# Retention and rational feed-forward on one core: a limit of three loads ahead on SyncE's queue, from the fifteenth load on

## The chip, the core and the metric

One core of a Trainium2 chip runs the whole program. The metric is the device time of one execution in microseconds (us); of several runs the median counts. The trace comes from one execution, taken by the hardware profiler.

## What is computed

The reference is decay-weighted attention without a softmax (retention), followed by a feed-forward layer whose activation is a quotient of a cubic and a quadratic. All is float32.

```python
# q, k, v: 8 batches, 8 heads, 576 positions, head size 64
gamma = 1.0 - 2.0 ** (-5.0 - np.arange(H))
rel = pos[:, None] - pos[None, :]
Dmat = np.where(rel >= 0, gamma[:, None, None] ** rel[None], 0.0)
x = ((q @ k.T) / 8 * Dmat) @ v          # (4608, 512) after the heads are joined
h = x @ w_in                            # 512 -> 2048
P = a[0] + a[1] * h + a[2] * h**2 + a[3] * h**3
Q = 1.0 + abs(b[0]) * abs(h) + abs(b[1]) * h**2
out = (P / (Q + 1e-6)) @ w_out          # 2048 -> 512
```

## The kernel before

The 4608 rows are cut into 36 **units** of 128 rows. A unit needs two loads: `qk` (queries and keys, 512 KB) and `kv` (keys and values, 512 KB; for units 0 to 3 only the values, 256 KB). Nine units make up two batches, and a state `S` is carried from unit to unit. The feed-forward layer works on nine blocks of 512 rows by sixteen slices of the hidden layer, one slice per **step**, 144 steps in all: `gemm1` (tiles `h`), the elementwise chain on ScalarE and VectorE (tiles `u`, `v`, `p`, `g`), then `gemm2` (tiles `acc`).

The weights come as 32 loads of 512 KB (`bits0_f` for slice f of `w_in`, `bits1_f` for slice f of `w_out`). Their words are taken apart and split into parts by ScalarE, VectorE and GpSimd some steps before a slice is first used.

Units 0 to 3 are worked on before the first step (`before(n)`), and unit 4 is begun there. After that a **visit** `visit(a, k)` finishes unit a and begins unit k: (4, 5) in step 0, (5, 6) in step 2, (6, 7) in step 4, the end of unit 7 in step 6, unit 8 from step 23 on, then a visit every two steps (24, 26, 28, 30) and from step 30 on every four. In a visit the matmuls read `qk` and `kv` of both units. Where the two halves of the TensorE array write one PSUM bank, the visit lets a matmul wait until the other half's matmuls are done. It does so through SyncE: an instruction that only waits is put on SyncE's queue and waits for TensorE, and a later matmul waits for it:

```python
            if n in after:
                seen[after[n]] = follow(nc.sync.nop(), ins)
```

So SyncE's queue holds three kinds of things, worked off strictly in order: the loads, the stores of finished output rows (`store`), and these waiting instructions (line 379). Each engine's own order is written out by hand in the tables `BEFORE0` and following. For SyncE it is not: its instructions come from the scheduler, which sets a load where it thinks that the load's buffer and semaphore are free.

The loads share eight semaphores in turn (`DMAHW0` to `DMAHW7`), so each DMA already waits until the DMA eight places ahead of it on the queue has landed.

The loads are called for in this order: constants, unit 0, masks, unit 1, mask, `bits0_0`, units 2 and 3, `bits0_1`, `bits0_2` (these are fourteen), then `bits0_3`, unit 4, `bits1_0`, `bits0_4`, unit 5, `bits1_1`, `bits0_5`, unit 6, and then two weights per step with the units between them as their buffers come free (`done_with`), until `bits1_15`; after that only units.

Of the kernel before, what the change touches and what calls it, by code (L numbers as in the profile page):

```python
# [21 lines left out]
P = 128  # L22
B, H, S, D = 8, 8, 576, 64
# [3 lines left out]
NPAIR = H // 2  # L27
# [44 lines left out]
VISITS |= {24 + 2 * i: (8 + i, 9 + i) for i in range(3)}  # L72
VISITS |= {30 + 4 * i: (11 + i, 12 + i if i < 24 else None) for i in range(25)}
WARM = "8 3 0 0 0 0 0 0 0".split()
LN_SHIFT = 60


# [12 lines left out]
def retention_ffn(ctx: ExitStack, tc: tile.TileContext, qkv, w_in, w_out, consts, masks, out):  # L90
# [10 lines left out]
    nc = tc.nc  # L101
# [19 lines left out]

    raws = {}

    def load_unit(n):


        late = 2 <= n < 6
        pools = [(wts, f"w{w}_{10 + n}") if late else (raw, "qk" if w == 0 else "kv") for w in range(2)]
        qk = pools[0][0].tile([P, 2, NPAIR, P], F32, tag=pools[0][1], name=f"qk{n}")
        nc.sync.dma_start(qk, qkv[n, :, 0:1024].rearrange("p (a g i) -> p a g i", a=2, g=NPAIR))  # L130
        kv = pools[1][0].tile([P, 2, H, D], F32, tag=pools[1][1], name=f"kv{n}")
        a = 1 if n < NP else 0
        nc.sync.dma_start(kv[:, a:], qkv[n, :, 1024 + 512 * a : 2048].rearrange("p (a h d) -> p a h d", h=H, d=D))
        raws[n] = qk, kv

    const_sb = const.tile([P, NPAIR * P + H + NPAIR + 6], F32, name="const_sb")
# [3 lines left out]
    mask_sb = const.tile([P, D], F32, name="mask_sb")  # L140
    firsts = op.tile([P, 2, DM], F32, tag="o0", name="whole_sb")[:, 0, 0 : 2 * P]
# [7 lines left out]
    def warm(n, by=None):  # L149
        by = gq_sb[:, 0] if by is None else by  # L150
        for _ in range(n):
            pe.matmul(unread[:, 0:P], by, by, start=True, stop=True)

    warm(int(WARM[0]), zeros)
    a0, a1, a2, a3 = (ab_sb[:, i : i + 1] for i in range(4))
# [4 lines left out]
    bits = {}  # L160
# [4 lines left out]
    def load_weight(k):  # L165

        bits[k] = wts.tile([P, DM], I64, tag=f"w{k[0]}_{k[1]}", name=f"bits{k[0]}_{k[1]}")
        nc.sync.dma_start(bits[k], (w_in, w_out)[k[0]][k[1]])

    def split_weight(k):  # L170

# [166 lines left out]
    def whole_outputs(n):  # L338
        q, v, o = raws[n][0][:, 0], raws[n][1][:, 1], sums_of(n)
        for j in range(2):  # L340
            ret = whole_ret(n, j)
            for c in range(2):
                for e in range(2):
                    pe.matmul(o[e * D : (e + 1) * D, j, c, :], v[:, 4 * c + 2 * e + j, :], ret[:, 2 * c + e, :], start=c == 0, stop=True, skip_group_check=True)
        if n % 9:
            for c in range(2):
                for j in range(2):
                    for e in range(2):
                        r = slice(j * D, j * D + D)
                        pe.matmul(o[e * D : (e + 1) * D, j, c, :], state[n][r, 2 * c + e, :], q[r, 2 * c + e, :], start=False, stop=True, skip_group_check=True)  # L350
# [30 lines left out]
    def follow(ins, earlier):  # L381
        how = mybir.DependencyInfo(mybir.DependencyClass.Sync, mybir.DependencyReason.DATA)
        tc.add_manual_dep(ins.ins, earlier.ins.name, how, reason="rows of the array that write one bank")
        return ins
# [20 lines left out]
    def done_with(a):  # L405

        del raws[a]
        state.pop(a, None)
        if 6 <= a + 2 < NU:
            load_unit(a + 2)  # L410
# [105 lines left out]
    def ffn_r(b, f):  # L516

        u, v, p = els[b, f]
        act.activation(u, v, AF.Ln, bias=math.ldexp(QC, -LN_SHIFT), scale=math.ldexp(1.0, -LN_SHIFT))
        act.activation(u, u, AF.Exp, bias=-LN_SHIFT * math.log(2.0), scale=-1.0)  # L520

# [132 lines left out]
    def load_weights(n):  # L654
        for k in [k for _, k in zip(range(n), loads)]:
            load_weight(k)
# [12 lines left out]
    def run(names, todo):  # L669
        todo |= {f"split{j}": (split_step, j) for j in range(4)}  # L670
        for name in names:
            if name in todo:
                todo[name][0](*todo[name][1:])

    def before(n):
        def outputs():
            if n == 1:
                nc.sync.dma_start(mask_sb, masks[:, 2 * P :])
            whole_outputs(n - 1)
            done_with(n - 1)  # L680
            load_more(n)

        todo = {"start": (split_start, int(STARTS_BEFORE[n]))}
        todo |= {f.__name__: (f, n + 1) for f in (scale_q, scale_v)}
        if n < NP:
            todo |= {"scores": (whole_scores, n), "state": (whole_state, n), "add": (whole_add, n), "fade": (fade, n)}
            todo |= {"decay": (whole_decay, n, 0), "decay1": (whole_decay, n, 1)}
            todo |= {"turn": (turn, n), "kn": (keep_turned, n)}
            todo["warm_a"] = warm, int(WARM[n + 1])
        else:  # L690
            todo |= {"scores": (visit, None, n), "decay": (decay, n), "add": (add, n), "fade": (fade, n)}
        if n >= 1:
            todo |= {f.__name__: (f, n - 1) for f in (keep_hi, keep_lo)}
            todo["outputs"] = (outputs,)
            if n < NP:
                todo["warm_b"] = warm, int(WARM[n + 5])
        run((BEFORE0, BEFORE1, BEFORE2, BEFORE3, BEFORE4)[n], todo)
# [4 lines left out]
    def load_more(n):  # L702


        for what in loading:
            if what == "|":
                return
            load_weights(1) if what == "weight" else load_unit(next(units))

    nc.sync.dma_start(const_sb, consts)  # L710
    load_unit(0)
    nc.sync.dma_start(firsts, masks[:, 0 : 2 * P])
    load_more(0)
    scale_q(0)
    scale_v(0)
# [12 lines left out]
    for i in range(len(steps) + lag(len(steps))):  # L728
# [4 lines left out]
        if i in VISITS:  # L733
            a, k = VISITS[i]
# [64 lines left out]
```

## Time and profile before

| | us |
|---|---|
| median of 3 runs | 868.04 |
| lowest and highest run | 867.76, 870.98 |
| the profiled execution | 871.07 |
| span of its trace | 869.0 |

The 2.07 us between the profiled execution's time and its span lie outside the instructions. The profiled execution is 3.03 us over the median.

### The profile page before, as it was taken

Reading aid. Unit: us, or ns where it says so; the run is one execution under the profiler, and the core shown is the slowest. Engines: PE = TensorE matmul, PEld = TensorE weight load, DVE = VectorE, ACT = ScalarE, POOL = GpSimd, SP = SyncE. Lnnn points to the kernel's source line nnn. Section 1 sums busy time; section 2 is a strip of 40 time slices with the busy share of each in tenths; the row PEclk is TensorE's granted clock in tenths of the full one; section 3 lists DMA queues with packets and bytes.
Section 4 is the critical chain, followed back from the end, with each engine's and each line's share of the span. In section 5 each row is a group of like instructions: output and inputs, shape, how many; then the busy total and the mean of one; then the engine's idle time right before and its main releaser. Section 6 shows DMA issues by size and latency. Waiting matters only on the chain.

```text
span 869.0 us, 18739 instructions
## 1 busy us (share of the span) xinstructions
PE 849.4 (98%) x7574; PEld 727.2 (84%) x7574; DVE 773.4 (89%) x1221; ACT 665.6 (77%) x1240; POOL 130.8 (15%) x107
## 2 busy tenths in 40 slices
PE   8899999999999999999999999999999999999997
PEld 6666787778888888888888888888888888888886
DVE  4998999999899889888889888888898988888995
ACT  3888999988767778777877787777877787767775
POOL 2523333631001110111111100011111111000000
PEclk9999999999999999999999999999999999999999
DMA  9896000032121112111211121101211121001001
GB/s 341 320 340 232 1 2 0 1 99 101 48 98 50 49 50 98 49 50 50 97 50 50 50 89 60 47 30 37 87 47 50 49 98 50 1 2 48 1 1 48
DMA packets 20774, 64.55 MB, mean 74 GB/s; under 512 B 2512, under 2 KB 2640, under 8 KB 20688
## 3 DMA queue, kind: packets, MB, share of 16 engines
q1 hardware_dynamic: 20528, 63.10, 20.6%
q8 instruction: 59, 0.97, 0.4%
q14 instruction: 27, 0.22, 0.1%
q10 hardware_dynamic: 160, 0.26, 0.1%
HBM read 53.91 MB, written 9.44 MB: 73 GB/s over the span
## 4 chain that ended last, share of the span: by engine, by line
PE 83%; DVE 10%; ACT 4%; issue 1%; DMA 1%; SPq 0%; POOL 0%; ACTq 0%; DVEq 0%; POOLq 0%
PE acc L86 39%; PE h L86 36%; DVE p L86 4%; PE ps L86 4%; DVE v L86 3%; PE y L86 2%; DVE c L86 1%; ACT free_at L86 1%; PE psNone L86 1%; DMA qk<-in_qkv 1%; ACT bits L86 1%; ACT g L86 1%; ACT c L86 0%; DVE qk L86 0%; ACT p L86 0%
## 5 line engine op out<-in xcount | busy, mean ns | idle before, releaser
L86 PE MATMUL h<-xhi,w 128*128 128x512 f32 x1152 | 367.8, 381 | 3.8 <-DVE p L86 1.9
L86 PE MATMUL acc<-w,g 128*128 128x512 f32 x1584 | 366.9, 381 | 3.0 <-ACT o L86 1.6
L86 PEld LDWEIGHTS acc<-w,g 128*128 128x128 f32 x1584 | 296.5, 189 | 47.6 <-ACT o L86 2.0
L86 PEld LDWEIGHTS h<-xhi,w 128*128 128x128 f32 x1152 | 217.7, 189 | 37.9 <-DVE p L86 3.1
L86 ACT ACTIVATE p<-h,const_sb 128x512 f32<-128x512 f32 x144 | 111.6, 775 | 165.0 <-PE h L86 158.4
L86 PE MATMUL h<-xlo,w 128*128 128x512 f32 x576 | 218.4, 379 | 0.1
L86 DVE TENSOR_TENSOR p<-p,h 128x512 f32<-128x512 f32 x144 | 98.6, 684 | 42.5 <-ACT u L86 40.1
L86 PEld LDWEIGHTS h<-xlo,w 128*128 128x128 f32 x576 | 108.9, 189 | 16.7 <-issue 1.1
L86 DVE SCALAR_TENSOR_TENSOR p<-p,const_sb,h 128x512 f32<-128x512 f32 x144 | 107.3, 745 | 4.0
L86 ACT ACTIVATE v<-u,absb 128x512 f32<-128x512 f32 x129 | 103.2, 800 | 0.4 <-DVE p L86 0.2
L86 DVE TENSOR_TENSOR v<-v,u 128x512 f32<-128x512 f32 x131 | 101.4, 774 | 0.2 <-ACT v L86 0.2
L86 DVE SCALAR_TENSOR_TENSOR p<-v,p 128x512 f32<-128x512 f32 x140 | 98.6, 704 | 3.3
L86 DVE SCALAR_TENSOR_TENSOR p<-p,const_sb,u 128x512 f32<-128x512 f32 x131 | 99.2, 758 | 1.2 <-ACT u L86 1.2
L86 POOL TENSOR_TENSOR S<-S,const_sb 128x256 f32<-128x256 f32 x32 | 27.2, 850 | 453.4 <-DVE S L86 453.4
L86 DVE SCALAR_TENSOR_TENSOR v<-v,u 128x512 f32<-128x512 f32 x131 | 89.4, 683 | 0.0
L86 ACT ACTIVATE u<-u 128x512 f32<-128x512 f32 x131 | 82.6, 630 | 4.3
L86 ACT ACTIVATE g<-p 128x512 fp32r<-128x512 f32 x132 | 82.8, 627 | 3.5 <-DVE p L86 3.0
L86 ACT ACTIVATE u<-v 128x512 f32<-128x512 f32 x131 | 81.9, 625 | 0.8 <-DVE v L86 0.8
L86 DVE TENSOR_TENSOR g<-p,g 128x512 fp32r<-128x512 f32 x115 | 78.6, 683 | 0.7 <-ACT g L86 0.7
L86 ACT ACTIVATE u<-h 128x512 f32<-128x512 f32 x131 | 76.7, 585 | 2.5 <-DVE v L86 2.4
L86 ACT ACTIVATE kv<-kv,const_sb 128x64 f32<-128x64 f32 x232 | 58.2, 333 | 4.5 <-DMA kv<-in_qkv 4.5
L86 POOL TENSOR_TENSOR qk<-qk,const_sb 128x512 f32<-128x512 f32 x31 | 48.6, 1566 | 38.8 <-DMA qk<-in_qkv 38.7
(93 smaller groups left out, 713.7 us busy)
## 6 DMA issues: line engine op xcount, KB each, us to landing
qk<-in_qkv SPq DMA_DIRECT2D x36, 512.0 KB, 4.1
kv<-in_qkv SPq DMA_DIRECT2D x32, 512.0 KB, 5.5
bits<-in_w_in SPq DMA_DIRECT2D x16, 512.0 KB, 8.1
bits<-in_w_out SPq DMA_DIRECT2D x16, 512.0 KB, 7.3
out<-o SPq DMA_DIRECT2D x28, 256.0 KB, 3.7
kv<-in_qkv SPq DMA_DIRECT2D x4, 256.0 KB, 7.0
out<-o SPq DMA_DIRECT2D x8, 128.0 KB, 2.1
out<-last SPq DMA_DIRECT2D x2, 256.0 KB, 2.4
```

Source lines behind the costliest of these rows:

```text
L86: return lambda *a, **k: self.tc.keep_in_program_order(method(*a, **k))
```

## The change

Every load, and only loads, goes through one helper. From the fifteenth call on, a load gets a dependence on the third load called for ahead of it: SyncE holds it back until that one has landed.

```diff
+AHEAD = 3
+FREE = 14
...
+    begun = []
+
+    def load(to, source):
+
+        begun.append(nc.sync.dma_start(to, source))
+        if len(begun) > FREE:
+            follow(begun[-1], begun[-1 - AHEAD])
+
...
-        nc.sync.dma_start(qk, qkv[n, :, 0:1024].rearrange("p (a g i) -> p a g i", a=2, g=NPAIR))
+        load(qk, qkv[n, :, 0:1024].rearrange("p (a g i) -> p a g i", a=2, g=NPAIR))
...
-        nc.sync.dma_start(bits[k], (w_in, w_out)[k[0]][k[1]])
+        load(bits[k], (w_in, w_out)[k[0]][k[1]])
```

The constants, the masks and `kv` go through it in the same way; the stores do not. `follow` (line 380) adds the dependence and is not changed.

**The first held-back loads.** On SyncE's queue, before, from the fourteenth load (`bits0_2`) to unit 5; the names in brackets are the semaphores that a row waits for:

```order
L168 DMA bits0_2_187<-in_w_in 128x512 [waits DMAHW5_49]
L168 DMA bits0_3_249<-in_w_in 128x512 [waits DMAHW6_49]
L130 DMA qk4_251<-in_qkv 128x1024 [waits DMAHW7_49]
L133 DMA kv4_253<-in_qkv 128x1024 [waits DMAHW0_49]
L168 DMA bits1_0_255<-in_w_out 128x512 [waits DMAHW1_49]
L168 DMA bits0_4_257<-in_w_in 128x512 [waits DMAHW2_49]
L130 DMA qk5_259<-in_qkv 128x1024 [waits DMAHW3_49]
L133 DMA kv5_261<-in_qkv 128x1024 [waits DMAHW4_49]
```

And the same place now, where all loads have the helper's line:

```order
L130 DMA bits0_2_187<-in_w_in 128x512 [waits DMAHW5_49]
L130 DMA bits0_3_249<-in_w_in 128x512 [waits DMAHW6_49,DMAHW3_49]
L130 DMA qk4_251<-in_qkv 128x1024 [waits DMAHW7_49,DMAHW4_49]
L130 DMA kv4_253<-in_qkv 128x1024 [waits DMAHW5_49,DMAHW0_49]
L130 DMA bits1_0_255<-in_w_out 128x512 [waits DMAHW6_49,DMAHW1_49]
L130 DMA bits0_4_257<-in_w_in 128x512 [waits DMAHW7_49,DMAHW2_49]
L130 DMA qk5_259<-in_qkv 128x1024 [waits DMAHW0_49]
L130 DMA kv5_261<-in_qkv 128x1024 [waits DMAHW1_49]
```

The order is the same here; `bits0_3` now also waits for `kv3`, `qk4` for `bits0_1`, `kv4` for `bits0_2`, and so on, each for the third ahead.

**The loads around the visit of step 4.** On SyncE's queue, before, from `bits0_8` on; a weight load that names `PE_49` stands right behind the waiting instructions of a visit:

```order
L168 DMA bits0_8_857<-in_w_in 128x512 [waits DMAHW3_49]
L168 DMA bits0_9_859<-in_w_in 128x512 [waits DMAHW4_49]
L168 DMA bits0_10_907<-in_w_in 128x512 [waits DMAHW5_49]
L168 DMA bits0_11_909<-in_w_in 128x512 [waits DMAHW6_49]
L168 DMA bits1_8_986<-in_w_out 128x512 [waits DMAHW7_49]
L168 DMA bits0_12_988<-in_w_in 128x512 [waits PE_49,DMAHW0_49,DVE_49]
L168 DMA bits1_9_1041<-in_w_out 128x512 [waits DMAHW1_49]
L130 DMA qk8_813<-in_qkv 128x1024 [waits DMAHW2_49,DVE_49,PE_49]
L133 DMA kv8_815<-in_qkv 128x1024 [waits DMAHW3_49,DVE_49,Pool_49]
```

And now:

```order
L130 DMA bits0_8_857<-in_w_in 128x512 [waits DMAHW2_49]
L130 DMA bits0_11_909<-in_w_in 128x512 [waits DMAHW3_49]
L130 DMA bits1_8_986<-in_w_out 128x512 [waits PE_49,DMAHW4_49]
L130 DMA qk8_813<-in_qkv 128x1024 [waits DMAHW0_49,DVE_49,PE_49]
L130 DMA kv8_815<-in_qkv 128x1024 [waits DMAHW1_49,DVE_49,Pool_49]
L130 DMA bits0_13_1043<-in_w_in 128x512 [waits DMAHW5_49]
L130 DMA bits0_9_859<-in_w_in 128x512 [waits DMAHW6_49]
L130 DMA bits0_10_907<-in_w_in 128x512 [waits DMAHW7_49]
L130 DMA bits1_11_1130<-in_w_out 128x512 [waits DMAHW0_49]
L130 DMA bits1_13_1183<-in_w_out 128x512 [waits DMAHW3_49,Activation_49]
L130 DMA qk9_962<-in_qkv 128x1024 [waits PE_49,DVE_49,DMAHW1_49,Pool_49]
```

Here loads have changed places: `bits0_9` and `bits0_10`, whose third load ahead is `qk8` and `kv8`, now stand behind that unit. The visit of step 6 has its waiting instruction between `bits1_13` and `qk9` now, and had it just ahead of `bits1_13` before.

**Who waits for SyncE.** On TensorE the order has not changed. In the visit (5, 6) of step 2 two matmuls wait for SyncE's waiting instructions, the second of them here (lines of the kernel before):

```order
L86 MATMUL ps5_6_569<-kv6_489 64x64 [waits SP_sequencer_49]
L86 MATMUL ps5_6_569<-kv6_489 64x64
L86 MATMUL y6_570<-kv6_489 64x64 x2
L86 MATMUL ps5_6_569<-kv6_489 64x64 x2
L86 MATMUL y6_570<-kv6_489 64x64 x2
L86 MATMUL ps5_6_569<-kv6_489 64x64 x2
L86 MATMUL y6_570<-kv6_489 64x64 x2
L86 MATMUL ps5_6_569<-kv6_489 64x64 x2
L86 MATMUL ps5_6_569<-qk5_259,kv5_261 64x64 [waits SP_sequencer_49]
```

On VectorE, ScalarE and GpSimd, too, the order is the same as before; only the numbers of the load semaphores differ.

## Rows read from the trace of the kernel before

**Rows 1.** The page: busy time by engine; DMA busy tenths in 40 slices.
```profile
PE 849.4 (98%) x7574; PEld 727.2 (84%) x7574; DVE 773.4 (89%) x1221; ACT 665.6 (77%) x1240; POOL 130.8 (15%) x107
DMA  9896000032121112111211121101211121001001
```

**Rows 2.** Waits (us, times, longest), whole span; the last three lie within 0-14 us.
```profile
POOL qk L86 <- DMA qk<-in_qkv: 38.7, 2, 19.4
...
POOL kv L86 <- DMA kv<-in_qkv: 10.9, 2, 9.4
...
DVE qk L86 <- DMA qk<-in_qkv: 8.4, 3, 4.6
...
ACT kv L86 <- DMA kv<-in_qkv: 4.5, 1, 4.5
```

**Rows 3.** Timeline of SyncE's queue: issue time, us, what (kv3, bits0_1 to 3, qk4, ...).
```profile
6.95 0.51 SPq L133 DMA_DIRECT2D kv<-in_qkv  x1
9.06 1.45 SPq L168 DMA_DIRECT2D bits<-in_w_in  x3
11.07 0.33 SPq L130 DMA_DIRECT2D qk<-in_qkv  x1
...
31.57 0.33 SPq L133 DMA_DIRECT2D kv<-in_qkv  x1
...
32.42 0.42 SPq L168 DMA_DIRECT2D bits<-in_w_in  x1
...
55.72 0.33 SPq L168 DMA_DIRECT2D bits<-in_w_in  x1
```

**Rows 4.** Landing, us after issue: windows around the six issues above; last two 230-860.
```profile
kv<-in_qkv SPq DMA_DIRECT2D x1, 256.0 KB, 8.4
...
bits<-in_w_in SPq DMA_DIRECT2D x1, 512.0 KB, 7.6
...
qk<-in_qkv SPq DMA_DIRECT2D x1, 512.0 KB, 9.8
...
kv<-in_qkv SPq DMA_DIRECT2D x1, 512.0 KB, 4.4
...
bits<-in_w_in SPq DMA_DIRECT2D x1, 512.0 KB, 6.4
...
bits<-in_w_in SPq DMA_DIRECT2D x1, 512.0 KB, 4.2
...
qk<-in_qkv SPq DMA_DIRECT2D x22, 512.0 KB, 4.0
kv<-in_qkv SPq DMA_DIRECT2D x22, 512.0 KB, 5.4
```

**Rows 5.** Timelines of VectorE and GpSimd: first uses of qk2, qk4, kv4, qk5, kv5.
```profile
12.33 0.69 DVE L86 TENSOR_TENSOR qk<-qk,const_sb 128x512 f32<-128x512 f32 x1 [1.04 <-DMA qk<-in_qkv]
...
21.45 1.73 POOL L86 TENSOR_TENSOR qk<-qk,const_sb 128x512 f32<-128x512 f32 x1
...
23.13 1.49 POOL L86 TENSOR_TENSOR kv<-kv,const_sb 128x512 f32<-128x512 f32 x1
25.99 0.93 POOL L86 TENSOR_TENSOR S<-S,const_sb 128x256 f32<-128x256 f32 x1 [1.37 <-DVE S L86]
...
28.57 0.68 DVE L86 TENSOR_TENSOR qk<-qk,const_sb 128x512 f32<-128x512 f32 x1
...
31.07 0.68 DVE L86 TENSOR_TENSOR kv<-kv,const_sb 128x512 f32<-128x512 f32 x1
```

**Rows 6.** TensorE's timeline at step 2; the chain that ended last at step 6.
```profile
42.91 0.67 PE L86 MATMUL ps<-qk,kv 64*64 64x64 f32 x16
...
71.14 0.02 SPq L379
```

**Rows 7.** SyncE's own waits, 20 to 76 us: for TensorE in the visits.
```profile
SPq L379 <- PE ps L86: 25.0, 5, 10.1
```

**Rows 8.** Timeline of ScalarE: first use of bits0_9.
```profile
98.01 0.86 ACT L86 ACTIVATE c<-bits 128x512 f32<-128x512 f32 x1
```

More of the change, by code (lines that the diff above doesn't have):

```diff
@@ L129, in load_unit @@
         qk = pools[0][0].tile([P, 2, NPAIR, P], F32, tag=pools[0][1], name=f"qk{n}")
-        nc.sync.dma_start(qk, qkv[n, :, 0:1024].rearrange("p (a g i) -> p a g i", a=2, g=NPAIR))
+        load(qk, qkv[n, :, 0:1024].rearrange("p (a g i) -> p a g i", a=2, g=NPAIR))
         kv = pools[1][0].tile([P, 2, H, D], F32, tag=pools[1][1], name=f"kv{n}")
         a = 1 if n < NP else 0
-        nc.sync.dma_start(kv[:, a:], qkv[n, :, 1024 + 512 * a : 2048].rearrange("p (a h d) -> p a h d", h=H, d=D))
+        load(kv[:, a:], qkv[n, :, 1024 + 512 * a : 2048].rearrange("p (a h d) -> p a h d", h=H, d=D))
         raws[n] = qk, kv
@@ L677, in outputs @@
             if n == 1:
-                nc.sync.dma_start(mask_sb, masks[:, 2 * P :])
+                load(mask_sb, masks[:, 2 * P :])
             whole_outputs(n - 1)
@@ L708, in load_more @@
             load_weights(1) if what == "weight" else load_unit(next(units))
-    nc.sync.dma_start(const_sb, consts)
+    load(const_sb, consts)
     load_unit(0)
-    nc.sync.dma_start(firsts, masks[:, 0 : 2 * P])
+    load(firsts, masks[:, 0 : 2 * P])
     load_more(0)
```

## The prediction

> **What bounds the kernel now.** I read the page first. TensorE is busy for 849.4 of 869.0 us, and VectorE for 773.4; the DMA engines are full only in the first four slices, some 87 us, and mostly below a third from then on [rows 1]. So a change of the loads can matter in two ways only: an engine waits for a load, or an engine waits for SyncE, whose queue holds the loads.
>
> The list of waits answers the first. Four lines name a load. Those of ScalarE, of VectorE, and of GpSimd for `kv` all lie in the first 14 us and are for units 0 to 2, whose loads are among the first fourteen and are not touched. The largest line, 38.7 us in two pieces, is GpSimd with nothing else to do (it is busy for 130.8 us in all) late in the kernel [rows 1, 2]. After 14 us nothing on the way to the end waits for a load. So there is no DMA wait to remove, and the question is how much room the loads have to be later.
>
> **What the change does to a load.** Before, up to eight loads are on their way. A load's landing is its issue [rows 3] plus its time to landing [rows 4]: kv3 lands at 6.95 + 8.4 = 15.35, bits0_1 at 9.06 + 7.6 = 16.66, qk4 at 11.07 + 9.8 = 20.87. Between bits0_1 and qk4 stand two more loads, so one of 512 KB lands every (20.87 - 16.66) / 3 = 1.40 us. The long time to landing of 8 to 10 us is therefore queueing behind the loads ahead: the engines take them one after the other. Holding a load back until two are ahead of it takes away waiting in the DMA queue and adds the same waiting on SyncE, as long as two loads keep the DMA engines busy while the third is being started.
>
> So one number decides, the time L from issue to landing with two loads ahead. The trace does not show it. From below: a load can land no faster than one issued alone, 4.0 us (22 times) to 4.4 us, and no faster than three paces, 4.2 us. From above: the third load of a burst that starts on idle engines took 6.4 us; the second of a pair took 5.4 us [rows 4]. The held-back loads run on engines that are already busy, one started as another lands, so I stay near the lower end and take **L = 4.4 us**.
>
> **The three places where L could cost something.**
>
> First, units 4 and 5. bits0_3 now starts when kv3 lands, bits1_0 when bits0_3 lands, kv5 when bits1_0 lands. kv5 lands at 15.35 + 3L, and VectorE wants it at 31.07 [rows 5]: it is late above L = 5.24. qk5 starts when kv4 lands, which started when bits0_2 landed (16.66 + 1.40 = 18.06); it lands at 18.06 + 2L and is wanted at 28.57, so late above 5.26. qk4 lands at 16.66 + L and GpSimd wants it at 21.45, kv4 at 18.06 + L and 23.13; beyond these GpSimd has 1.37 us of idle time before its next `S` [rows 5], so they hurt above 6.1 and 6.4. With L = 4.4 kv5 lands at 28.55, and 2.5 us are left. Cost: nothing. The cover is VectorE's other work; without it kv5 would cost 3 us for each us of L.
>
> Second, the visit of step 2. Its two waiting instructions on SyncE stand behind loads, and matmuls stand behind them. The second is behind bits1_4, which now waits for bits0_7, which waits for bits1_2. kv6 lands at 31.57 + 4.4 = 35.97 and bits0_6 at 32.42 + 6.4 = 38.82 [rows 3, 4]; bits1_2 lies between them, at about 37.4. So bits1_4 is issued at 37.4 + L, and the matmul that needs it starts at 42.91 [rows 6]: late above L = 5.5. With 4.4 it is 41.8, 1.1 us early. The first waiting instruction is behind kv7, which waits for bits1_3; that is issued at 35.97 + L, which has more room.
>
> Third, step 6. The waiting instruction now stands behind bits1_13, which waits for bits1_11, which waits for bits0_13, which waits for bits1_8; and bits1_8 is the first load behind the visit of step 4, where 55.72 stands now. It lands at 55.72 + 4.2 = 59.92 [rows 3, 4], so bits1_13 goes out at 59.92 + 2L. SyncE's wait for the visit ends at 71.14 [rows 6]: late above L = 5.6. With 4.4 it is 68.7, and 2.4 us are left. SyncE stood for 25.0 us in five such waits between 20 and 76 us [rows 7]; that is where the new waits for loads go.
>
> **The rest.** bits0_9 and bits0_10 are moved behind unit 8. qk8 is issued within about 1 us of bits1_8 and lands by about 55.72 + 1 + 5.4 = 62; bits0_9 then by about 67, and ScalarE first uses it at 98.01 [rows 8]. The last weights hang in a chain of five loads behind the visit of step 6 and land by about 71.14 + 5 x 4.4 = 93; all that stands behind bits0_9 is used after it. From unit 10 on, units are called for two or four steps apart; a step is about 869 / 144 = 6.0 us, a little less without the head of the kernel, so some 11 us lie between a load and the third ahead of it, and loads there land in 4.0 and 5.4 us [rows 4]: the wait is met before it is reached. Queued behind the loads on SyncE are also the stores; they go out where the wait costs nothing. No other engine gets or loses an instruction.
>
> **Sum.** 0 + 0 + 0 on the profiled execution's 871.07 us (span 869.0 and 2.07 outside it). The median of the runs is 868.04, 3.03 below that execution; the same sum on it gives **868.0 us**.
>
> **A rule against it.** The Trainium skill, "DMA: Bandwidth & Descriptors", section "Rules for kernel authors", says to issue a load early and wait for it late, so that its fixed cost is hidden; this change issues loads later. The section "Anatomy of one DMA" of the same page puts a load at about 2.0 us plus its bytes at 436 GB/s (fitted on GpSimd's path); were the 2.0 us added in full to three transfers of 1.20 us, L would be 5.6 by that estimate, and the time 869.2 us. The trace agrees with a fixed part of that order (4.0 us alone against a pace of 1.40), but no row shows it added to loads in a queue.
>
> **Rivals.** (1) *Slower: the held-back loads restart the engines each time.* Then L is as in the burst, 6.4 us [rows 4]. kv5 is late by 3 x 6.4 + 15.35 - 31.07 = 3.5 us; the visit of step 2 by 37.4 + 6.4 - 42.91 = 0.9 more; step 6 by 59.92 + 12.8 - 71.14 = 1.6 more: 6.0 us, 874.0 us. It begins at L = 5.24. The three terms together are 6L - 32.4, so the loss passes 0.5% (4.3 us) at L = 6.1. For it speaks that 6.4 is the only row with two loads ahead and a near-empty queue; against it the pace of 1.40 with a full one. (2) *Faster: the first loads land sooner*, because those behind them no longer share the engines. VectorE waited 1.04 us for qk2 [rows 5]; that is all there is to win: 867.0 us. Against it speaks that loads land in order and at an even pace. (3) Something that no row shows, in either direction.
>
> **How the numbers follow.** This kernel's runs tell about 0.5% from no change. Chances: the forecast 0.80, rival 1 0.12 (half of it over 0.5%), rival 2 0.02, unseen 0.06 (0.04 faster, 0.02 slower). So faster 0.04, slower 0.06 + 0.02 = 0.08, the rest, 0.88, within 0.5%. The range reaches from rival 2 with half a microsecond of scatter, 866.5, to 872.0, which takes in rival 1 up to about L = 6.06 and the highest run, 870.98.
>
> **What would show it.** Right: loads from the fifteenth on land 4 to 5 us after their issue instead of 8 to 10; no wait for `kv5` on VectorE; SyncE waits less for TensorE and now for loads; TensorE's matmuls at step 2 and step 6 start within some tenths of 42.91 and 71.2; the DMA engines stay busy some 10 us longer. Wrong: VectorE waiting for kv5 near 31 us, TensorE waiting for SyncE at step 2 or 6, or a landing time near 6 us.

## The result: 0.8% slower, and the profile after

Six runs of each kernel, taken beside each other, gave a median of 876.77 us after (874.42 to 879.10) against 869.00 us before (867.76 to 871.40): a ratio of 1.0083 (95%: 1.0060 to 1.0107), so some 7.2 us slower (7.8 by the medians). The forecast of 868.0 us was wrong, and its range, which ended at 872.0, did not hold the result. The profiled execution of after took 877.29 us with a span of 875.3, 6.3 us longer than the span before; those 6.3 us are what the traces can explain.

The page of after: busy time by engine, the tenths of the DMA engines in 40 slices, and the chain's shares.

```profile
PE 849.1 (97%) x7574; PEld 726.6 (83%) x7574; DVE 766.6 (88%) x1221; ACT 666.4 (76%) x1240; POOL 131.3 (15%) x107
...
DMA  8867500014121112111211112111211121001001
...
PE 77%; DVE 9%; DMA 8%; ACT 4%; issue 1%; SPq 0%; POOL 0%; ACTq 0%; DVEq 0%; POOLq 0%
```

TensorE did the same work in the same time (849.1 us against 849.4, [rows 1]); it idles more. The DMA engines are now less full in the first four slices and busy in a fifth one: the same bytes over a longer stretch. And 8% of the chain of work that ended last are now transfers, where it was 1% before.

The chain shows where. These are its pieces from 19 to 78 us (start, us, what); the short pieces between them are left out.

```profile
19.09 5.95 DMA kv<-in_qkv
...
25.06 4.94 DMA qk<-in_qkv
...
30.01 5.43 DMA bits<-in_w_in
...
35.45 6.09 DMA bits<-in_w_out
...
41.56 4.61 DMA bits<-in_w_in
...
46.18 5.25 DMA bits<-in_w_out
...
51.45 4.88 DMA bits<-in_w_out
...
56.34 3.66 DMA bits<-in_w_in
...
60.02 3.72 DMA bits<-in_w_in
...
63.76 4.01 DMA bits<-in_w_out
...
67.79 4.14 DMA bits<-in_w_in
...
71.95 4.96 DMA bits<-in_w_out
...
77.35 0.02 SPq L389
...
77.41 0.46 PE ps_None L88 x16
```

From 19 to 77 us one load hands over to the next: each starts as the one before it in the chain lands. The last of them, `bits1_11`, lands at 76.92; then SyncE reaches the waiting instruction of the visit of step 6, and TensorE's matmul, which waits for that, starts at 77.41. SyncE's wait there ended at 71.14 before [rows 6] and ends at 77.35 now: 6.2 us later, which is nearly the whole loss of this execution (6.3 us). Nothing is lost behind it.

The list of waits from 14 to 80 us (us, times, longest one) names the engines that paid:

```profile
PEld ps L88 <- SPq L389: 4.0, 4, 2.4
PE ps L88 <- SPq L389: 3.4, 3, 2.3
POOL kv L88 <- DMA kv<-in_qkv: 3.1, 2, 2.3
DVE qk L88 <- DMA qk<-in_qkv: 2.4, 1, 2.4
...
POOL qk L88 <- DMA qk<-in_qkv: 1.6, 1, 1.6
...
PE ps_None L88 <- SPq L389: 1.2, 1, 1.2
DVE kv L88 <- DMA kv<-in_qkv: 0.6, 1, 0.6
```

There are two kinds. Engines wait for the loads of units 4 and 5 themselves, and TensorE waits for SyncE's queue (line 389 is the visit's waiting instruction, line 379 before). Of [rows 2], every load wait that mattered lay in the first 14 us; these are new.

On TensorE's timeline (start, us, what, the idle time before it and what ended that) the loss can be followed. The milestones are four first matmuls of `acc`: those behind the visits of steps 2, 4 and 6, and, third, those of the step between the last two visits:

```profile
33.63 0.27 PE L88 MATMUL y<-kv 64*64 64x64 f32 x2 [2.13 <-DVE kv L88]
...
46.62 0.46 PE L88 MATMUL ps<-qk,kv 64*64 64x64 f32 x16 [0.69 <-SPq L389]
47.01 4.58 PE L88 MATMUL acc<-held,g 128*128 128x512 f32 x8
...
60.46 0.27 PE L88 MATMUL ps<-kv 64*64 64x64 f32 x2 [2.26 <-SPq L389]
61.31 4.58 PE L88 MATMUL acc<-held,g 128*128 128x512 f32 x8
...
68.32 4.48 PE L88 MATMUL acc<-held,g 128*128 128x512 f32 x8
...
77.41 0.46 PE L88 MATMUL ps_None<-qk,kv 64*64 64x64 f32 x16 [1.16 <-SPq L389]
77.80 4.58 PE L88 MATMUL acc<-held,g 128*128 128x512 f32 x8
```

The same milestones before:

```profile
43.51 5.48 PE L86 MATMUL acc<-held,g 128*128 128x512 f32 x8
...
56.13 4.58 PE L86 MATMUL acc<-held,g 128*128 128x512 f32 x8
...
63.14 4.49 PE L86 MATMUL acc<-held,g 128*128 128x512 f32 x8
...
71.59 4.58 PE L86 MATMUL acc<-held,g 128*128 128x512 f32 x8
```

TensorE is behind by 3.5, 5.2, 5.2 and 6.2 us: unit 5 and step 2 first (2.13 and 0.69 us of waiting, and 0.40 at the visit of step 0), then step 4 (2.26), then step 6 (1.16).

Not all of the first 3.5 us is waiting. TensorE's granted clock fell behind the idle 2.13 us: from 36 to 38 us it was 0.50, the lower of the two levels (1.2 GHz), and matmuls of `h` took 0.63 us where they take 0.38 at the full clock. The kernel before had such a stretch too, behind 2.05 us of idle time before 41.76, and its matmuls at the first milestone took 5.48 us in place of 4.58. A window of after and one of before (stretch, length, busy time of PE, PEld, DVE, ACT and POOL with instructions, granted clock, DMA share, GB/s):

```profile
34.00:40.00 6.00, 5.58 (x55) 4.46 (x46) 5.61 (x10) 1.62 (x3) 2.92 (x3) 0.72 0.85 286
```
```profile
42.00:48.00 6.00, 6.00 (x87) 3.31 (x80) 6.00 (x13) 5.68 (x11) 3.62 (x3) 0.72 0.98 362
```

In this pair of executions the two nearly cancel: when the visit of step 4 begins, TensorE is 2.6 us behind (56.70 against 54.11).

### The profile page after: what moved, and what is told of

It reads as the page before. It is cut to its first block, busy times and chain, and to the rows that moved or that the text cites. A ratio compares the mean times of both kernels' runs of the same rounds, so it can differ in the third digit from the quotient of the medians.

```text
span 875.3 us, 18739 instructions
## 1 busy us (share of the span) xinstructions
PE 849.1 (97%) x7574; PEld 726.6 (83%) x7574; DVE 766.6 (88%) x1221; ACT 666.4 (76%) x1240; POOL 131.3 (15%) x107
## 4 chain that ended last, share of the span: by engine, by line
PE 77%; DVE 9%; DMA 8%; ACT 4%; issue 1%; SPq 0%; POOL 0%; ACTq 0%; DVEq 0%; POOLq 0%
PE acc L88 37%; PE h L88 35%; DVE p L88 4%; PE ps L88 4%; DMA bits<-in_w_in 4%; DMA bits<-in_w_out 3%; DVE v L88 3%; PE y L88 2%; DMA kv<-in_qkv 1%; DVE c L88 1%; ACT free_at L88 1%; DMA qk<-in_qkv 1%; ACT bits L88 0%; ACT g L88 0%; ACT c L88 0%
## 5 line engine op out<-in xcount | busy, mean ns | idle before, releaser
L88 PEld LDWEIGHTS h<-xhi,w 128*128 128x128 f32 x1152 | 218.4, 190 | 37.4 <-DVE p L88 3.1
L88 POOL TENSOR_TENSOR S<-S,const_sb 128x256 f32<-128x256 f32 x32 | 36.1, 1128 | 449.2 <-DVE S L88 428.2
L88 DVE TENSOR_TENSOR v<-v,u 128x512 f32<-128x512 f32 x131 | 95.0, 725 | 0.2 <-ACT v L88 0.2
L88 POOL TENSOR_TENSOR qk<-qk,const_sb 128x512 f32<-128x512 f32 x31 | 41.7, 1345 | 41.1 <-DMA qk<-in_qkv 41.1
```

The source lines that it names most:

```text
L88: return lambda *a, **k: self.tc.keep_in_program_order(method(*a, **k))
```

## Two theories

**R, the rate.** A load held back until two are ahead of it takes longer than 4.4 us to land, because three loads under way do not keep the DMA engines full. Every load from the fifteenth on gets later and later.

**Q, the order in the queue.** `load` counts in the order of its calls; SyncE's queue is in the order that the scheduler made. `qk8` and `kv8` are called for between `bits1_7` and `bits0_8`, but stand further behind in the queue (the second pair of listings in the section on the change). So the load that `bits0_8` waits for, the third ahead by call, is `bits1_7`, the one directly ahead of it in the queue. `bits0_11` waits in the same way for `bits0_8`, and `bits1_8` for `bits0_11`. The chain shows it: 51.45, 56.34, 60.02, 63.76, each of the last three going out only as the one before it lands.

The experiments undo one or the other, or remove one of the two ways by which late loads reach an engine. Edits are against the kernel after unless said otherwise; each was run beside the kernel before, and ratios are to that.

## Experiments: rate or order

**Four ahead in place of three.**

```diff
-AHEAD = 3
+AHEAD = 4
```

> AHEAD = 4 in place of 3. Theory R (rate): with three loads under way the DMA engines move only some 275 GB/s in place of 415, because a load needs 5 to 6 us from issue to landing however few are ahead of it; every load from the fifteenth on is late, and with it unit 5 and the visits of steps 0, 2, 4 and 6. With four under way the rate is 4 x 524 KB / 5.6 us = 375 GB/s: 869 to 872 us, bits0_3 to bits0_5 spaced 1.4 us, not 1.9. Theory Q (queue order): units 8 and 9 are called for ahead of weights that stand before them on the queue, so that the third load ahead by call is the one directly ahead on the queue, and six weight loads go one at a time ahead of the visits of steps 4 and 6; that alone makes the loss. With AHEAD = 4 they go two at a time: 871 to 874 us, and the delay appears only at steps 4 and 6.

Measured: 874.41 us against 869.65, ratio 1.0066 (1.0046 to 1.0085), above both ranges. TensorE now keeps up until step 4: the first matmuls of `acc` behind the visits of steps 2 and 4 start at 41.54 and 53.26 us. Then, in the list of waits from 14 to 90 us:

```profile
PE ps_None L88 <- SPq L389: 5.1, 1, 5.1
```

This one wait, at step 6, is as large as the whole loss. So R's losses up to step 4 go away with one more load under way, and what stays is in the stretch where the queue's order differs.

**Loads 15 to 35 alone held back**, and **loads from the 38th (`bits0_8`) on alone**.

```diff
-        if len(begun) > FREE:
+        if FREE < len(begun) <= 35:
```

> The limit holds for the loads 15 to 35 alone (bits0_3 to bits1_7); from unit 8 on it is gone, and the queue is in the order of before. Theory R: unit 5 and the visit of step 2 are late as in the changed kernel, step 4 is not much better since the loads ahead of it start late: 872 to 875 us, TensorE's first matmul with kv5 near 33.6 us in place of 31.8. Theory Q: no load stands in another's way out of order: 868.5 to 870 us.

```diff
-FREE = 14
+FREE = 37
```

> The limit holds from the thirty-eighth load on (bits0_8), so the first loads go as before and the six weight loads still go one at a time. Theory R: the chain of six starts at about 50 us, not at 56, and at 3.7 to 5 us a load the waiting instruction of step 6 is reached at about 70.8, just before 71.14: 868.5 to 871 us. Theory Q: the chain is the loss: 873 to 877 us.

Measured: the first part 873.52 us, ratio 1.0049 (1.0030 to 1.0068); the second 871.29, 1.0019 (1.0003 to 1.0035). In the first part, TensorE waits 1.40 us for `kv5` by way of VectorE and 2.34 us for SyncE at step 2, and nothing in the stretch of Q; in the second it waits 1.22 us at step 6 alone. Both stretches cost, the early one more. R's range held the first and missed the second by 0.3 us; Q's ranges missed both. The second run is the one in which Q meets loads that are on time: it costs 0.19% there.

**Units 8 and 9 neither counted nor held back**, which gives the queue the order that it had before, so that Q is gone.

```diff
-    def load(to, source):
+    def load(to, source, counted=True):
...
-        begun.append(nc.sync.dma_start(to, source))
+        one = nc.sync.dma_start(to, source)
+        if not counted:
+            return
+        begun.append(one)
```

(the calls for units 8 and 9 pass `n not in (8, 9)`)

> AHEAD = 3 from the fifteenth load on, but units 8 and 9 are neither counted nor held back, so that the queue has the order of before and the third ahead by call is the third ahead on the queue. Theory R: steps 0 and 2 are as late as in the changed kernel, the waiting instructions of step 4 stand behind bits0_8 to bits0_11 and bits1_8 at 1.9 us each, near 60 us: 873 to 876 us. Theory Q: 868.5 to 870.5 us.

Measured: 877.15 us, ratio 1.0090 (1.0073 to 1.0106): as slow as the changed kernel, 1 us above R's range and far above Q's. The waits for SyncE moved forward: 1.01 us at step 2 and 2.00 us at step 4, in place of 0.69 and 2.26, and at step 6 no more than 0.3. The four milestones start at 46.47, 61.21, 69.47 and 77.91 us, the last as late as the 77.80 of after. From the second to the third it takes 8.26 us where after takes 7.01, at a granted clock of 0.50 from 62 to 64 us and 0.65 from 64 to 66, behind the 2.00 us of idle time. So with three ahead the loss comes without Q: late loads, the waits that they cause and the lower clock behind these waits are enough for it. It is not the changed kernel with Q taken away and all else left alone, since in the old order five loads of this stretch stand ahead of step 4's waiting instructions and not two.

**Both: four ahead, and units 8 and 9 not counted.**

```diff
-AHEAD = 3
+AHEAD = 4
...
+        if not counted:
+            return
```

> AHEAD = 4, and units 8 and 9 neither counted nor held back, so the queue has the order of before. With four ahead, the run before this one showed steps 0 to 4 on time and 5.1 us of TensorE's time lost at step 6 alone. If that loss is the queue order (the third or fourth load ahead by call standing directly ahead on the queue), it goes, and the time is that of before: 868 to 871 us, with less than 0.5 us of waiting for SyncE at step 6. If it is the rate that four loads reach, the waiting stays: 872 to 875 us.

Measured: 869.20 us against 869.43, ratio 0.9995 (0.9982 to 1.0008). Nothing is lost. With four ahead, the order in the queue (with the hold on units 8 and 9 that makes it) was therefore the whole cause. With three, R alone is enough (0.90%), and Q behind loads that are on time costs 0.19%.

## Experiments: by which way the late loads reach TensorE

**The visits' waiting instructions on GpSimd's queue** in place of SyncE's, so that no load stands ahead of them; and the same edit **on the kernel before** as a control.

```diff
-                seen[after[n]] = follow(nc.sync.nop(), ins)
+                seen[after[n]] = follow(nc.gpsimd.nop(), ins)
```

> The changed kernel, with the visits' waiting instructions on GpSimd's queue and not on SyncE's, so that a held-back load holds up nothing but later loads. If the loss is passed on through SyncE's waiting instructions (0.4 + 0.7 + 2.3 + 1.2 us at steps 0, 2, 4 and 6 in the changed kernel), it falls to unit 5's late landing, some 2 us: 870 to 873 us. If late weights or units hold the other engines up by themselves, it stays: 875 to 878 us.

> The control for the run with the waiting instructions on GpSimd's queue: the kernel before with that edit alone. TensorE waited for SyncE in two visits for 0.3 us each, so nothing is to be won: 868 to 871 us. If GpSimd's own work is held up by the visits, slower, 871 to 874 us.

Measured: 872.75 us, ratio 1.0035 (1.0016 to 1.0053), and 869.62, 1.0006 (0.9991 to 1.0022) for the control. The loads are as late as in after, the move of the waiting instructions is by itself worth nothing, and yet, by the two ratios, more than half of the loss goes: that part was the waiting instructions standing behind loads. What is left is unit 5: VectorE waits 1.70 us for `qk5`, TensorE 1.40 us for `kv5`. Against the trace of the control, `kv5`'s first matmul is 0.83 us late (33.34 and 32.51) and the first milestone 1.68 (45.51 and 43.83), and it stays at 1.68. The second half of it is the clock behind the wait; the same window of this run and of the control:

```profile
34.00:40.00 6.00, 5.30 (x36) 4.34 (x28) 5.38 (x10) 1.98 (x4) 3.99 (x4) 0.72 0.85 268
```
```profile
34.00:40.00 6.00, 5.87 (x57) 4.97 (x60) 5.93 (x10) 3.77 (x7) 3.99 (x4) 1.00 1.02 418
```

**Loads 15 to 21 alone held back (up to `kv5`)**, and **the rest alone, from the 22nd (`bits1_1`) on.**

```diff
-        if len(begun) > FREE:
+        if FREE < len(begun) <= 21:
```

> AHEAD = 3 for the loads 15 to 21 alone (bits0_3 to kv5). If unit 5's late landing is a loss of its own, TensorE starts with kv5 some 1 to 2 us late and stays so: 870 to 872 us, with the visits of steps 2 to 6 not waiting for SyncE by more than 0.5 us. If the loss of the first part is all at the visits' waiting instructions, 868.5 to 870 us.

```diff
-FREE = 14
+FREE = 21
```

> AHEAD = 3 from the twenty-second load on (bits1_1), so unit 5 lands as before and all later loads are held back as in the changed kernel. The loss to unit 5 alone was measured at 2.1 us, that of the whole change at 7.5 us. If the parts add, this one costs 4 to 6 us: 873 to 876 us, all of it in waits for SyncE at steps 2, 4 and 6. If the late unit 5 is what starts the later losses, 869 to 872 us.

Measured: 871.56 us, ratio 1.0033 (1.0019 to 1.0047), and 873.55, 1.0044 (1.0022 to 1.0066). 0.33% and 0.44% add to 0.77%, which lies in the interval of the whole change. The profiled run of the first is a mild one (869.86 us; 0.34 us of waiting for `qk5`, 0.27 for `kv5`), so its half rests on its timed runs. In the second, units 4 and 5 are on time and TensorE's waits for SyncE stand alone. From its list of waits from 14 to 90 us, and SyncE's wait of step 6 in its chain:

```profile
PEld ps L88 <- SPq L389: 4.1, 2, 3.3
PE ps L88 <- SPq L389: 3.8, 2, 3.2
```
```profile
76.11 0.02 SPq L389
```

So the sum is not a division of one path: with the first 21 loads left free, SyncE's wait of step 6 still ends at 76.11 us, 1.24 earlier than in after.

**Both ways closed:** from the 22nd load on, and the waiting instructions on GpSimd.

```diff
-FREE = 14
+FREE = 21
...
-                seen[after[n]] = follow(nc.sync.nop(), ins)
+                seen[after[n]] = follow(nc.gpsimd.nop(), ins)
```

> AHEAD = 3 from the twenty-second load on, and the visits' waiting instructions on GpSimd's queue: the limit stays for 86 loads, but neither way is left by which it was seen to cost time (unit 5's landing; waiting instructions behind held-back loads). If these two are the whole loss, 869 to 870.5 us, within 0.2% of the kernel before. If late weights or late units also cost by themselves, 871 us or more.

Measured: 869.96 us against 869.48, ratio 1.0010 (0.9991 to 1.0028). Every load from the 22nd on is still held back at three, and no loss is left that can be told from none. No cost of late loads by themselves shows here, up to the 0.28% of the interval; they cost where unit 5 wants them and where SyncE's waiting instructions stand behind them.

## Experiments: the time to landing with one and two under way

The edit of the fourth experiment (units 8 and 9 not counted) with `AHEAD = 2`, and with `AHEAD = 1`; one execution each.

> AHEAD = 2, units 8 and 9 not counted: how long a load takes with one load ahead of it. If loads under way slow each other from the second on (3.7 to 4.1 us alone, 4.9 to 6 with three under way, 10 with eight), some 4.6 us, 2.3 us from landing to landing and 230 GB/s between 20 and 50 us. If a load waits only for those ahead to be moved, and its own part is fixed, as the prediction had it, 4.0 to 4.2 us, 2.1 us and 250 GB/s. Time either way some 885 to 892 us.

> AHEAD = 1, units 8 and 9 not counted: one counted load at a time, which gives the time of a load alone on idle engines, 3.7 to 4.1 us by the single-file loads of the changed kernel, 4.0 us by those of units before; 125 to 140 GB/s. The waiting instruction of step 6 is reached after some 34 such loads, near 145 us: 935 to 950 us.

Measured: 891.92 and 902.56 us, the kernel before 869.79 beside them. Windows of 20 to 50 us (stretch, length, busy time of PE, PEld, DVE, ACT and POOL with instructions, granted clock, DMA share, GB/s) for, in turn, `AHEAD` of 1, 2, 3 (the kernel after) and 4 (the first experiment), and up to eight under way (the kernel before):

```profile
20.00:50.00 30.00, 15.83 (x258) 12.79 (x251) 11.87 (x20) 11.37 (x21) 7.62 (x7) 0.72 0.45 147
```
```profile
20.00:50.00 30.00, 22.73 (x396) 18.33 (x392) 21.08 (x37) 20.84 (x37) 11.09 (x10) 0.88 0.74 233
```
```profile
20.00:50.00 30.00, 23.13 (x410) 17.59 (x411) 23.29 (x41) 21.86 (x38) 12.14 (x12) 0.94 0.84 279
```
```profile
20.00:50.00 30.00, 26.02 (x431) 19.83 (x424) 26.75 (x46) 25.78 (x46) 14.51 (x12) 1.00 0.94 337
```
```profile
20.00:50.00 30.00, 25.76 (x436) 19.13 (x435) 28.19 (x47) 26.17 (x46) 15.94 (x13) 0.94 0.88 334
```

The last column is the curve that the prediction lacked: 147, 233, 279, 337 GB/s. With eight the mean of the stretch is held down by SyncE's waits for the visits, which leave it no load to issue for some time; from 15 to 20 us that kernel moved 416 GB/s. The times to landing of the weight loads from `w_out` in the same stretch (count, KB each, median us), for one, two, three and four under way:

```profile
bits<-in_w_out SPq DMA_DIRECT2D x2, 512.0 KB, 3.5
```
```profile
bits<-in_w_out SPq DMA_DIRECT2D x4, 512.0 KB, 4.6
```
```profile
bits<-in_w_out SPq DMA_DIRECT2D x6, 512.0 KB, 5.4
```
```profile
bits<-in_w_out SPq DMA_DIRECT2D x7, 512.0 KB, 6.2
```

The two views agree: three loads of 524 kB in 5.4 us are 291 GB/s, two in 4.6 us are 228, one in 3.5 us is 150. With two, the figures of the first theory came out (4.6 us, 230 GB/s).

The time with `AHEAD = 1` missed its expectation of 935 to 950 us by far. The waiting instruction of step 6 came at 101.3 us and not at 145, because the scheduler, given so long a chain, moved loads: those of units 8 and 9 ahead of weights, and many weights behind the visit of step 6. A chain worked out by hand holds only as long as the queue keeps its order.

## Why the prediction was wrong, step by step

**What held.** There was no wait for a load to win; rival 2 did not show. The three places named, units 4 and 5, step 2 and step 6, are places where the loss arose, beside step 4 and a little at step 0. For units 4 and 5 the bounds of L were right: VectorE waits for `qk5` and `kv5`, as L passed 5.26 and 5.24 (`qk5`'s chain also began 1 us late, `bits0_2` landing at 19.02 where 18.06 was reckoned). For steps 2 and 6 they were not (second failed step). The late weights and everything behind step 6 cost nothing. SyncE does wait for loads now, as its own waits from 14 to 100 us show:

```profile
SPq L130 <- DMA bits<-in_w_out: 23.2, 11, 4.6
SPq L130 <- DMA bits<-in_w_in: 20.6, 13, 3.3
...
SPq L130 <- DMA qk<-in_qkv: 13.0, 6, 5.6
```

**First failed step: L = 4.4 us.** The seventeen held-back loads from `qk4` to `bits1_4` landed 4.4 to 7.0 us after their issue, with a median of 5.4. In windows round single issues, `qk4`, `kv4`, `bits1_0` and `kv5`:

```profile
qk<-in_qkv SPq DMA_DIRECT2D x1, 512.0 KB, 5.0
...
kv<-in_qkv SPq DMA_DIRECT2D x1, 512.0 KB, 6.0
...
bits<-in_w_out SPq DMA_DIRECT2D x1, 512.0 KB, 7.0
...
kv<-in_qkv SPq DMA_DIRECT2D x1, 512.0 KB, 5.4
```

`kv5` went out at 27.35 and landed at 32.75, where 28.55 was forecast: VectorE started it at 32.80 and not at 31.07 [rows 5]. The reasoning behind 4.4 was that waiting moves from the DMA queue to SyncE one for one, since loads are taken one after the other. The runs show that they overlap instead: of the 5.4 us that a load takes with two ahead, 3.5 are there when it is alone, and each load ahead adds only 0.8 to 1.1 us where the pace of a full queue is 1.26 (524 kB at 416 GB/s) to 1.40. Taking one away therefore saves less waiting than one pace, and the difference is lost rate: 279 GB/s in the stretch in place of 416 at the full queue. I had the warning in [rows 4] (4.0 us alone against a pace of 1.40) and chose the bound nearer to the pace. Rival 1 had L pass the bounds, at 6.4, which was too high. But this step alone does not make the loss: at the measured L of 5.4 the prediction's own three terms give 0.5 us (3 x 5.4 + 15.35 - 31.07 for `kv5`, and nothing at steps 2 and 6).

The estimate that the Trainium skill ("DMA: Bandwidth & Descriptors", section "Anatomy of one DMA") gave in the prediction, 5.6 us for three, was nearer than mine to the 5.4 measured. These runs agree that a part of a load's time is not hidden by two loads ahead, though each load adds less than that estimate's 1.20 us. The time that it gave, 869.2 us, was nearly as far off as mine, because the next step was wrong in it too.

**Second failed step: the starts of the chains, above all 55.72 as the issue of `bits1_8`.** This is where most of the loss was missed. The prediction read from the new order that `bits1_13` waits for `bits1_11`, that for `bits0_13`, and that for `bits1_8`, which is so; but it took the start of this chain from the trace of before. With its terms: `bits1_8` was issued at 63.76 in place of 55.72 (8.04 late) and landed in 4.0 us in place of 4.2; two more loads took 9.15 us in place of 8.8. Their sum ends at 76.92 us in place of 68.7. The 2.4 us of room are used up, and SyncE's wait ends at 77.35 in place of 71.14. Nearly all of this is the first term, and that is what stands ahead of `bits1_8`: `bits0_8` and `bits0_11`, which the order in the queue makes go singly, behind loads that L had made late. At step 2 the same was done: the landing of `bits1_2`, 37.4 by the trace of before, came at 41.54, and `bits1_4` went out at 46.18 in place of 41.8.

The chain in the section on the result shows what to follow instead. From the landing of `bits0_2` to the issue of `bits1_13` twelve loads go one after the other (`kv4`, `qk5`, `bits0_5`, `bits1_2`, `bits0_7`, `bits1_4`, `bits1_7`, `bits0_8`, `bits0_11`, `bits1_8`, `bits0_13`, `bits1_11`). With the prediction's 18.06 for that landing, `bits1_4` goes out at 18.06 + 5L, late above L = 4.97, and `bits1_13` at 18.06 + 12L, late above L = 4.42. The forecast's 4.4 left 0.3 us there and not 2.4. Measured, the twelve took 57.9 us from 19.02 on, 4.82 each.

**Third failed step: places left out.** The visit of step 4 was not costed, nor the waiting instructions of step 0 (0.40 us). Step 4's waiting instructions stand behind `bits0_8` and `bits0_11`, and TensorE waited 2.26 us for them. The prediction used that visit only as a starting time. The lower clock behind such waits was in no term either.

**What each is worth.** By the timed runs, holding back the loads up to unit 5 alone costs 0.33% (2.9 us), and holding back the rest alone 0.44% (3.8 us), of the 0.83% of the change. A part of each is a lower granted clock. The kernel before, run beside the experiments, took a span of 866.5 us on average in 22 executions with a mean granted clock of 1.000, and 869.5 us in five with 0.995. The mean clock was 0.9965 and 0.9962 in the two experiments, and 0.9984 and 0.9979 in the kernel before beside them: some 1.1 us of each loss, an estimate from these rows. How much of the 2.26 us at step 4 is R and how much Q in the changed kernel is not settled: without Q it was 2.00 us, but from another start. That rival 1's 6.0 us came so near to the measured 7.2 is chance, since step 4, the lateness carried from one place to the next and the order in the queue were in none of its terms.

## What to carry to other kernels

A limit on loads under way is a limit on the rate: divide bytes under way by the measured time to landing at that number, and compare with what the stretch needs, rather than assume that waiting only moves from one queue to another. Follow one chain of held-back loads from its start to each place that waits, since a time read from the old trace is itself made late by the loads ahead of it. List what else stands on the queue that will wait; here hand-shakes for TensorE stood behind the loads, and moving them to another queue took away more than half of the loss. Count "the third ahead" in the order that the queue has after scheduling, for a dependence on a load that ended up directly ahead makes these loads go one at a time.

## What the runs showed of the hardware

Loads of 512 KB on SyncE's queue overlap more than their even landings suggest. One alone lands in 3.5 us, and with two, three and four under way it takes 4.6, 5.4 and 6.2 us, so the rate rises less than the number under way: 147, 233, 279 and 337 GB/s. With up to eight, 416 GB/s is reached (15 to 20 us of the kernel before). I had read the even pace of 1.40 us of a full queue as the time that a load needs by itself; it is the pace of several at once, and four under way still stay below it.

A wait of TensorE cost more than its length where the granted clock fell behind it: with the waiting instructions on GpSimd, 0.83 us of late start became 1.68, at a granted clock of 0.72 from 34 to 40 us where the control had 1.00.
